# Subtracting query maxima on TensorE, in a reordered attention loop: what it does to a fused attention and spectral-mixing kernel

## The chip, the cores and the metric

The kernel runs on one core of a Trainium2 chip. The metric is device microseconds (us) of one execution. A profiled execution also has a span, from its first to its last instruction, some 1.7 us under its own time. Calls ran on different chips, so a comparison across calls is weaker than one within a call.

## The reference

Condensed:

```python
def phi(x):                                   # q, k: (8, 8, 576, 64); w_phi: (64, 128)
    proj = np.einsum('bhsd,df->bhsf', x, w_phi)
    proj = proj - np.max(np.abs(proj), axis=-1, keepdims=True)
    return np.concatenate([np.exp(proj), np.exp(-proj)], axis=-1)
kv  = einsum(phi(k), v);  z = sum(phi(k))     # per batch and head
x   = (phi(q) @ kv) / (phi(q) @ z + 1e-6)     # heads side by side: (8, 576, 512)
X   = rfft(x, axis=1)[:, :64]                 # 64 modes, each times its own complex 512x512 matrix
u   = x + irfft(mixed X);  out = u + relu(u @ w_ch)
```

The 128 mode matrices (real and imaginary) are 134 MB in HBM as fp32; they are the bulk of what the kernel reads (163.6 MB). Note that `np.exp(-proj)` is taken after the subtraction of the maximum m, so the two halves are exp(p - m) and exp(-p + m). The kernel before makes exp(p) and exp(-p) of the queries and multiplies one of the two sums by exp(2m), as a common factor cancels between numerator and denominator; the changed one makes exp(p - m) and exp(-p + m) directly.

## The kernel before

Attention is cut into 16 units (two heads, two batches each). One unit's work for its queries:

```python
def rows_q(self, i):                # projections, rows on partitions; DVE reduces the absolute maximum
    m = self.mq
    self.rows(self.qT, i, m[:, :, 4 * i:4 * i + 4] if i < 2 else m[:, :, 8])

def exp_mq(self):                   # exp(2m), four small ACT instructions
    self.e2 = pm.tile([128, 2, 9], F32, name="e2")
    ...
def cols_q(self, i): ...            # projections again, features on partitions: two PSUM banks
def exp_q(self, i): ...             # ACT: exp(p) and exp(-p) of them

def num(self, n0):                  # six of 18 row groups; three calls a unit
    pn = [None, None]
    for ab in (1, 0):               # one PSUM group for each sign
        pn[ab] = one([128, 6, 65])
        ... pe.matmul(pn[ab][...], lhsT=AQ, rhs=kvz, start=True, stop=True)
    nd = pm.tile([128, 6, 65], F32, name="nd")
    dve.tensor_tensor(out=nd, in0=pn[1], in1=<e2 broadcast>, op=ALU.mult)
    dve.tensor_tensor(out=nd, in0=pn[0], in1=nd, op=ALU.add)
    dve.reciprocal(rd, nd[:, :, 64])
    dve.tensor_tensor(out=xs[...], in0=nd[:, :, 0:64], in1=<rd broadcast>, op=ALU.mult)
```

The loop runs unit Q (numerators), K (keys' projections, query transposes and maxima) and R (key transposes) at once, and from pass n = 4 on mixes weights in between (condensed):

```python
Q.cols_q(0); Q.exp_q(0); K.rows_k(0); K.exp_k(0)
Q.kv(); Q.cols_q(1); Q.exp_q(1); P.freq()                 # P: spectrum of the unit before Q
if n == 4: some(2)                                        # some(k): k weights' mixing matmuls
Q.num(0); K.turn_q(); K.rows_k(1); K.exp_k(1); some(min(X, 2))
Q.num(6); Q.cols_q(2); Q.exp_q(2); some(min(X - 2, 2))
K.rows_k(2); K.exp_k(2); K.weigh_v(); K.rows_q(0); K.rows_q(1); K.rows_q(2)
R.turn_k(); K.weigh_v2(); Q.num(12); K.exp_mq(); some(X - 4)
```

All engines keep program order. Weights are loaded as bf16 by transfers that GpSimd issues, 1 MB each, into 13 places at first (8 rotating buffers and 5 borrowed tiles); each `some` step that frees a rotating buffer issues the next one:

```python
def wload(g, w):
    wt = home(g, w)                                       # one of the 13 places
    pool.dma_start(wt, (moe_w_r, moe_w_i)[i][MG * o:MG * o + MG, ...])
def some(n):
    for _ in range(n):
        mix(*key, wts.pop(key), ...)                      # 8 matmuls
        if key not in held: next_w(1)                     # the place is free: issue the next weight
```

After attention come the inverse tables (about 20 us of VectorE, PE idle), then the rest of the mixes among channel products and sums, and last the output stage.

Of the kernel before, what the change touches and what calls it, by code (L numbers as in the profile page):

```python
# [10 lines left out]
F32 = mybir.dt.float32  # L11
# [32 lines left out]
def kernel(  # L44
# [42 lines left out]
    pm = pm_cm.__enter__()  # L87

# [8 lines left out]
    class Unit:  # L97
# [15 lines left out]
        def turn(self, src, name, flat):  # L113

            dst = pm.tile([128, 9, 128], BF16, name=name, tag="xT", bufs=3)
            rows = src.rearrange("p i c d -> p (i c d)")
            for lo, hi in ((0, 4), (4, 9)):
                ptr = one([128, hi - lo, 128], BF16)
                for j in range(lo, hi):
                    if flat or j < 4:  # L120
                        pe.transpose(ptr[:, j - lo, :], rows[:, j * 128:(j + 1) * 128], ident_b)
                    elif j < 8:
                        n = 9 + 2 * (j - 4)
                        pe.transpose(ptr[:, j - lo, :], rows[:, n * 64:n * 64 + 128], ident_b)
                    else:
                        for i in range(2):
                            pe.transpose(ptr[64 * i:64 * i + 64, j - lo, :], src[:, i, 8, :], ident_b)
                act.copy(dst[:, lo:hi, :], ptr)
            return dst

        def turn_k(self):
            self.kT = self.turn(self.kb, "kT", True)
            self.mk = pm.tile([128, 2, 18], F32, name="mk")

        def turn_q(self):
            self.qT = self.turn(self.qb, "qT", False)
            self.mq = pm.tile([128, 2, 9], F32, name="mq")
# [21 lines left out]
        def exp_k(self, i):  # L159
            if i == 0:  # L160
                self.AB = []
            if i < 2:
                t = pm.tile([128, 2, 8, 128], BF16, name="AB", bufs=3)
            else:
                t = pm.tile([128, 2, 2, 128], BF16, name="ABr")
            for ab in range(2):
                act.activation(t[:, ab], self.pk, ACT.Exp, scale=1.0 - 2.0 * ab)
            self.AB.append(t)
# [18 lines left out]
        def kv(self):  # L187
            pk = [one([128, 2, 2, 65]) for h in range(2)]
            for i in range(2):
                for ab in range(2):  # L190
                    for c in range(9):
                        n = 9 * i + c
                        for h in range(2):
# [5 lines left out]
                            )  # L199
            for h in range(2):  # L200
                act.copy(self.kvz[:, h], pk[h])

        def rows_q(self, i):
            m = self.mq
            self.rows(self.qT, i, m[:, :, 4 * i:4 * i + 4] if i < 2 else m[:, :, 8])

        def exp_mq(self):
            self.e2 = pm.tile([128, 2, 9], F32, name="e2")
            for h in range(2):
                for a in range(2):  # L210
                    act.activation(self.e2[64 * a:64 * a + 64, h, :], self.mq[64 * h:64 * h + 64, a, :],
                                   ACT.Exp, scale=2.0)

        def cols_q(self, i):

            if i < 2:
                ps = two([128, 2, 4, 128])
                for c2 in range(2):
# [4 lines left out]
                        start=True, stop=True,  # L223
                    )
            else:
                ps = one([128, 2, 128])
                for h in range(2):
                    pe.matmul(ps[:, h, :], lhsT=w2blk[:, h * 128:(h + 1) * 128],
                              rhs=self.qT[:, 8, :], start=True, stop=True)
            self.pa = ps  # L230

        def exp_q(self, i):
            if i == 0:
                self.AQ = []
            if i < 2:
                t = pm.tile([128, 2, 2, 2, 2, 2, 64], BF16, name="AQ")
            else:
                t = pm.tile([128, 2, 2, 128], BF16, name="AQr")
# [9 lines left out]
        def num(self, n0):  # L248

            pn = [None, None]  # L250
            for ab in (1, 0):
                pn[ab] = one([128, 6, 65])
                for n in range(n0, n0 + 6):
                    h = n % 2
                    if n < 16:
                        i, c = n // 8, n % 8 // 2
                        pe.matmul(
                            pn[ab][:, n - n0, :],
                            lhsT=self.AQ[i][:, ab, c % 2, c // 2, h].rearrange("f a p -> f (a p)"),
                            rhs=self.kvz[:, h, i, ab, :], start=True, stop=True,  # L260
                        )
                    else:
                        for i in range(2):
                            r = slice(64 * i, 64 * i + 64)
                            pe.matmul(
                                pn[ab][r, n - n0, :],
                                lhsT=self.AQ[2][:, ab, i, 64 * h:64 * h + 64],
                                rhs=self.kvz[:, h, i, ab, :], start=True, stop=True,
                            )
            nd = pm.tile([128, 6, 65], F32, name="nd")  # L270
            dve.tensor_tensor(
                out=nd.rearrange("p (k h) d -> p k h d", h=2),
                in0=pn[1].rearrange("p (k h) d -> p k h d", h=2),
                in1=self.e2[:, :, n0 // 2:n0 // 2 + 3].rearrange("p h k -> p k h").unsqueeze(3)
                .to_broadcast([128, 3, 2, 65]), op=ALU.mult,
            )
            dve.tensor_tensor(out=nd, in0=pn[0], in1=nd, op=ALU.add)
            rd = pm.tile([128, 6], F32, name="rd")
            dve.reciprocal(rd, nd[:, :, 64])
            dve.tensor_tensor(  # L280
                out=xs[:, self.g, self.bp, n0:n0 + 6, :], in0=nd[:, :, 0:64],
# [3 lines left out]
        def freq(self):  # L285
            g, bp = self.g, self.bp
            px = one([128, 4, 2, 64])
            for i in range(2):
                for c in range(5):
# [5 lines left out]
                    )  # L295
            act.copy(
# [50 lines left out]
    dve.tensor_copy(ident_b, ident_f)  # L347
    units[0].load_q()
# [17 lines left out]
    units[0].turn_k()  # L366
# [83 lines left out]
    units[2].load_k()  # L450
    for n in range(-1, len(units) + 1):
        def unit(i):
            return units[i] if 0 <= i < len(units) else None

# [374 lines left out]
```

## Time and profile before

| what | before |
|---|---|
| time, median of 3 (lowest to highest) | 482.02 us (479.99 to 482.52) |
| span of the profiled run, granted clock | 478.6 us, 0.852 |
| busy: PE, VectorE, ScalarE | 338, 314, 293 us |
| attention ends (first mix after it) | 320.1 us |
| last packet of the last weight | 423.1 us |
| matmuls of the last weight | 434.65 us |

How to read it: there are two things that can set the end. One is the row of work: attention, tables, rest, each as fast as its engines pass work on. The other is the row of transfers, which is nearly full from the start; the last weight must have landed before its matmuls, and what follows those matmuls takes 44 us. In the kernel before the row of work was the later one, by 434.65 - 423.1 = 11.5 us. The last mix has no wait for a weight:

```profile
434.65 0.69 PE L37 MATMUL pt<-wt,XT 128*32 128x512 bf16 x8
```

### The profile page before, as it was taken

How to read it: one execution, taken by the hardware profiler on the slowest of the kernel's cores; microseconds unless marked ns; L12 is line 12 of the kernel's file. 1: busy time of each engine (PE TensorE's matmuls, PEld its weight loads, DVE VectorE, ACT ScalarE, POOL GpSimd, SP SyncE). 2: the span in 40 equal slices, each digit the busy share in tenths (PEclk: the TensorE clock that was granted, in tenths of full speed). 3: DMA queues.
4: the chain of work that ended last, by engine and by line, in shares of the span. 5: the costliest groups of instructions: out<-in, count | busy, mean ns of one | idle time of the engine just before them, and what ended most of it. 6: DMA issues, size and time to landing. Idle time of an engine off the chain costs nothing.

```text
span 478.6 us, 9253 instructions
## 1 busy us (share of the span) xinstructions
PE 337.9 (71%) x3738; PEld 201.4 (42%) x3780; DVE 313.8 (66%) x547; ACT 292.8 (61%) x524; POOL 92.7 (19%) x130
## 2 busy tenths in 40 slices
PE   1566666747776667867877777650499995999991
PEld 1354444535454454544554554430255541333330
DVE  5368768739588778788696696647533331775782
ACT  4566867857769777767658767501244542666671
POOL 5222210104113202212122021050012120000331
PEclk9998888589789888788588597785699997999996
DMA  8999999968999999999999999999999999931797
GB/s 193 207 228 209 227 227 213 222 142 129 229 214 223 228 227 208 229 219 217 228 207 228 228 207 207 205 189 207 207 207 213 214 218 217 207 75 45 216 326 250
DMA packets 86299, 99.23 MB, mean 207 GB/s; under 512 B 2800, under 2 KB 79728, under 8 KB 86256
## 3 DMA queue, kind: packets, MB, share of 16 engines
q0 software_dynamic: 77264, 81.80, 100.0%
q1 hardware_dynamic: 8992, 16.85, 11.2%
q8 instruction: 29, 0.48, 0.4%
q14 instruction: 14, 0.11, 0.1%
HBM read 163.64 MB, written 9.44 MB: 362 GB/s over the span
## 4 chain that ended last, share of the span: by engine, by line
DVE 35%; issue 28%; PE 21%; ACT 7%; POOL 5%; DMA 3%; POOLq 0%; DVEq 0%; ACTq 0%
PE pt L37 12%; DVE va L37 7%; PE one L37 7%; DVE mq L37 7%; DVE mk L37 6%; DVE nd L37 6%; ACT AB L37 4%; DVE xs L37 3%; DMA qb<-in_q_dram 3%; PE two L37 2%; POOL wt L37 2%; POOL out_dram L37 2%; DVE zall L37 2%; ACT kvz L37 2%; DVE rd L37 1%
## 5 line engine op out<-in xcount | busy, mean ns | idle before, releaser
L37 ACT ACTIVATE AB<-two 128x1024 bf16<-128x1024 f32 x64 | 62.0, 1021 | 55.3 <-DVE mk L37 55.3
L37 ACT CAST xw<-pt 128x512 bf16<-128x512 f32 x72 | 42.1, 587 | 44.9 <-PE pt L37 43.8
L37 ACT ACTIVATE AQ<-two 128x1024 bf16<-128x1024 f32 x64 | 62.7, 1043 | 0.7 <-PE two L37 0.3
L37 DVE TENSOR_TENSOR nd<-one,e 128x390 f32<-128x390 f32 x48 | 26.7, 557 | 54.4 <-PE one L37 54.4
L37 PE MATMUL one<-kvz,AQ 128*128 128x65 bf16 x512 | 33.8, 214 | 31.0 <-ACT kvz L37 21.6
L37 PE MATMUL pt<-wchb,xT 128*128 128x512 bf16 x136 | 36.9, 385 | 20.0 <-DVE xT L37 19.7
L37 PE MATMUL one<-va,AB 64*128 64x65 bf16 x1024 | 29.9, 216 | 26.4 <-DVE va L37 26.1
L37 PEld LDWEIGHTS <-AQ 128*128 128x128 bf16 x512 | 28.5, 111 | 45.4 <-issue 43.5
L37 DVE TENSOR_REDUCE mk<-two 128x8 f32<-128x1024 f32 x32 | 39.0, 1220 | 10.1 <-PE two L37 9.9
L37 POOL DMA_DIRECT2D wt<-in_moe_w_r_dram x29 | 25.6, 883 | 85.5 <-PE one L37 63.2
L37 DVE TENSOR_TENSOR va<-vn,ee 128x1152 bf16<-128x1152 f32 x32 | 41.9, 1352 | 0.0
L37 POOL DMA_DIRECT2D qb<-in_q_dram x16 | 11.4, 712 | 154.1 <-PE one L37 154.1
L37 PEld LDWEIGHTS <-AB 64*128 64x128 bf16 x1024 | 25.8, 111 | 32.6 <-DVE va L37 18.0
L37 PEld LDWEIGHTS <-xs 128*128 128x128 bf16 x304 | 29.2, 112 | 24.4 <-issue 11.4
L37 DVE TENSOR_REDUCE mq<-two 128x8 f32<-128x1024 f32 x32 | 37.7, 1217 | 1.4 <-PE two L37 1.4
L37 DVE TENSOR_TENSOR xs<-pt,xs 128x512 bf16<-128x512 f32 x36 | 24.3, 691 | 18.3 <-PE pt L37 17.9
L37 POOL DMA_DIRECT2D wt<-in_moe_w_i_dram x30 | 26.5, 882 | 44.9 <-PE pt L37 43.6
L37 PEld LDWEIGHTS <-XT 128*32 128x32 bf16 x512 | 20.1, 173 | 29.7 <-issue 20.5
L37 PE MATMUL one<-CF,xs 128*128 128x256 bf16 x160 | 29.3, 344 | 4.4 <-DVE xs L37 2.8
L37 DVE COPY xT<-pt 128x512 bf16<-128x512 bf16 x36 | 15.1, 422 | 26.2 <-PE pt L37 26.2
L37 DVE TENSOR_TENSOR nd<-one,nd 128x390 f32<-128x390 f32 x48 | 27.1, 565 | 5.4 <-DVE nd L37 0.5
L37 PE MATMUL one<-wt,XT 128*32 128x512 bf16 x296 | 26.4, 486 | 4.2 <-ACT yacc L37 2.4
(107 smaller groups left out, 652.2 us busy)
## 6 DMA issues: line engine op xcount, KB each, us to landing
wt<-in_moe_w_i_dram POOLq DMA_DIRECT2D x30, 1024.0 KB, 20.9
wt<-in_moe_w_r_dram POOLq DMA_DIRECT2D x29, 1024.0 KB, 18.7
vn<-in_v_dram SPq DMA_DIRECT2D x16, 576.0 KB, 7.6
kb<-in_k_dram POOLq DMA_DIRECT2D x16, 288.0 KB, 20.6
qb<-in_q_dram POOLq DMA_DIRECT2D x16, 288.0 KB, 13.1
out_dram<-of SPq DMA_DIRECT2D x16, 256.0 KB, 5.3
out_dram<-of POOLq DMA_DIRECT2D x16, 256.0 KB, 5.0
yacc<-in_moe_w_r_dram POOLq DMA_DIRECT2D x1, 1024.0 KB, 12.0
```

The source lines that it names most:

```text
L37: ins = f(*args, **kwargs)
```

## The change

The intent is to take work off VectorE. The query maximum is split into three bf16 parts (high 16 bits of m, of the remainder, of its remainder), transposed by TensorE, and subtracted from the projections in PSUM by a matmul with minus one. Both exponentials then carry the right factor, so their two products with the key sums accumulate in one PSUM group, and VectorE only divides. The loop is reordered and starts one pass earlier: query transposes and the first query columns are now made one pass ahead of where they were.

```diff
+        def shift_q(self):
+            high = self.m3.bitcast(BF16).rearrange("p t (n s) -> p t n s", s=2)[:, :, :, 1]
+            for t in range(2):
+                dve.tensor_tensor(out=self.m3[:, t + 1, 0:18], in0=self.m3[:, t, 0:18],
+                                  in1=high[:, t, 0:18], op=ALU.subtract)
+            pt = one([96, 128], BF16)
+            pe.transpose(pt, high.rearrange("p t n -> p (t n)"), ident_b)
+            self.mT = pm.tile([96, 128], BF16, name="mT")
+            act.copy(self.mT, pt)
+        def shifted(self, out, n, stop):
+            pe.matmul(out, lhsT=minus[:, n:n + 1].to_broadcast([96, 128]), rhs=self.mT,
+                      start=False, stop=stop)
         def cols_q(self, i):
...
-                        start=True, stop=True,
+                        start=True, stop=False,
                     )
+                    for j in range(4):
+                        self.shifted(ps[:, c2, j, :], 8 * i + 2 * j + c2, j == 3)
...
         def num(self, n0):
-            (two groups, then nd = pn[1] * e2, nd = pn[0] + nd: see above)
+            pn = one([128, 6, 65])      # ab = 0 starts the group, ab = 1 adds to it
+            dve.reciprocal(rd, pn[:, :, 64])
+            dve.tensor_tensor(out=xs[...], in0=pn[:, :, 0:64], in1=<rd broadcast>, op=ALU.mult)
...
-    for n in range(-1, len(units) + 1):
-        X = 0 if n < 4 else 6 if n == 4 else 4 if n % 2 else 2
+    for n in range(-2, len(units) + 1):
+        X = 0 if n < 4 else 6 if n == 4 else 3 if n % 2 else 2
+        Q.exp_q(0); K.rows_k(0); K.exp_k(0); Q.weigh_v2(); P.freq(); P.keep_x()
+        if n == 4: some(2)
+        Q.cols_q(1); Q.exp_q(1); some(1 if X else 0); K.rows_k(1); K.exp_k(1)
+        Q.kv(); K.rows_q(0); K.rows_k(2); K.rows_q(2); K.rows_q(1)
+        Q.cols_q(2); Q.keep_kv(); Q.exp_q(2); K.exp_k(2); K.weigh_v(); some(1 if X else 0)
+        K.shift_q(); Q.num(0); K.cols_q(0); R.turn_k(0); R.turn_k(1)
+        Q.num(6); R.turn_q(0); R.turn_q(1); Q.num(12); some(X - 2)
+        if n < 3: next_w((1, 3, 3, 2, 2)[n + 2])
```

(The loop is condensed; loads and the guards for missing units are cut.)

More of the change, by code (lines that the diff above doesn't have):

```diff
@@ L87 @@
     pm = pm_cm.__enter__()
+    m3s = [pm.tile([128, 3, 32], F32, name=f"m3{i}", bufs=1) for i in range(2)]
+    minus = pm.tile([96, 32], BF16, name="minus", bufs=1)
     def load(t, src, g, bp, eng):
@@ L111, in load_v, with turn @@
             load(self.vn, v, self.g, self.bp, sp)
-        def turn(self, src, name, flat):
-            dst = pm.tile([128, 9, 128], BF16, name=name, tag="xT", bufs=3)
+        def turn(self, src, dst, flat, part):
             rows = src.rearrange("p i c d -> p (i c d)")
-            for lo, hi in ((0, 4), (4, 9)):
-                ptr = one([128, hi - lo, 128], BF16)
-                for j in range(lo, hi):
-                    if flat or j < 4:
-                        pe.transpose(ptr[:, j - lo, :], rows[:, j * 128:(j + 1) * 128], ident_b)
-                    elif j < 8:
-                        n = 9 + 2 * (j - 4)
-                        pe.transpose(ptr[:, j - lo, :], rows[:, n * 64:n * 64 + 128], ident_b)
-                    else:
-                        for i in range(2):
-                            pe.transpose(ptr[64 * i:64 * i + 64, j - lo, :], src[:, i, 8, :], ident_b)
-                act.copy(dst[:, lo:hi, :], ptr)
-            return dst
@@ L131, in turn_k @@
-        def turn_k(self):
-            self.kT = self.turn(self.kb, "kT", True)
-            self.mk = pm.tile([128, 2, 18], F32, name="mk")
-        def turn_q(self):
-            self.qT = self.turn(self.qb, "qT", False)
-            self.mq = pm.tile([128, 2, 9], F32, name="mq")
+            lo, hi = ((0, 4), (4, 9))[part]
+            ptr = one([128, hi - lo, 128], BF16)
+            for j in range(lo, hi):
+                if flat or j < 4:
+                    pe.transpose(ptr[:, j - lo, :], rows[:, j * 128:(j + 1) * 128], ident_b)
+                elif j < 8:
+                    n = 9 + 2 * (j - 4)
+                    pe.transpose(ptr[:, j - lo, :], rows[:, n * 64:n * 64 + 128], ident_b)
+                else:
+                    for i in range(2):
+                        pe.transpose(ptr[64 * i:64 * i + 64, j - lo, :], src[:, i, 8, :], ident_b)
@@ new lines, in turn, with turn_k, turn_q @@
+            act.copy(dst[:, lo:hi, :], ptr)
+        def turn_k(self, part):
+            if part == 0:
+                self.kT = pm.tile([128, 9, 128], BF16, name="kT", bufs=2)
+                self.mk = pm.tile([128, 2, 18], F32, name="mk")
+            self.turn(self.kb, self.kT, True, part)
+        def turn_q(self, part):
+            if part == 0:
+                self.qT = pm.tile([128, 9, 128], BF16, name="qT", bufs=3)
+                self.m3 = m3s[self.bp % 2]
+            self.turn(self.qb, self.qT, False, part)
@@ L164, in exp_k @@
             else:
-                t = pm.tile([128, 2, 2, 128], BF16, name="ABr")
+                t = pm.tile([128, 2, 2, 128], BF16, name="ABr", bufs=1)
             for ab in range(2):
@@ L199, in kv, with keep_kv @@
                             )
+            self.pk2 = pk
+        def keep_kv(self):
             for h in range(2):
-                act.copy(self.kvz[:, h], pk[h])
+                act.copy(self.kvz[:, h], self.pk2[h])
         def rows_q(self, i):
-            m = self.mq
-            self.rows(self.qT, i, m[:, :, 4 * i:4 * i + 4] if i < 2 else m[:, :, 8])
-        def exp_mq(self):
-            self.e2 = pm.tile([128, 2, 9], F32, name="e2")
-            for h in range(2):
-                for a in range(2):
-                    act.activation(self.e2[64 * a:64 * a + 64, h, :], self.mq[64 * h:64 * h + 64, a, :],
-                                   ACT.Exp, scale=2.0)
+            self.rows(self.qT, i, self.m3[:, 0, 8 * i:min(8 * i + 8, 18)])
+        def shift_q(self):
[10 more added lines that the diff above has]
+                      start=False, stop=stop)
         def cols_q(self, i):
@@ L228, in cols_q @@
                     pe.matmul(ps[:, h, :], lhsT=w2blk[:, h * 128:(h + 1) * 128],
-                              rhs=self.qT[:, 8, :], start=True, stop=True)
+                              rhs=self.qT[:, 8, :], start=True, stop=False)
+                    self.shifted(ps[:, h, :], 16 + h, True)
             self.pa = ps
@@ L235, in exp_q @@
             if i < 2:
-                t = pm.tile([128, 2, 2, 2, 2, 2, 64], BF16, name="AQ")
+                t = pm.tile([128, 2, 2, 2, 2, 2, 64], BF16, name="AQ", bufs=3)
             else:
-                t = pm.tile([128, 2, 2, 128], BF16, name="AQr")
+                t = pm.tile([128, 2, 2, 128], BF16, name="AQr", bufs=1)
             for ab in range(2):
@@ L248, in num @@
         def num(self, n0):
-            pn = [None, None]
-            for ab in (1, 0):
-                pn[ab] = one([128, 6, 65])
-                for n in range(n0, n0 + 6):
-                    h = n % 2
-                    if n < 16:
-                        i, c = n // 8, n % 8 // 2
+            pn = one([128, 6, 65])
+            for n in range(n0, n0 + 6):
+                h = n % 2
+                if n < 16:
+                    i, c = n // 8, n % 8 // 2
+                    for ab in range(2):
@@ L257, in num @@
                         pe.matmul(
-                            pn[ab][:, n - n0, :],
+                            pn[:, n - n0, :],
                             lhsT=self.AQ[i][:, ab, c % 2, c // 2, h].rearrange("f a p -> f (a p)"),
-                            rhs=self.kvz[:, h, i, ab, :], start=True, stop=True,
+                            rhs=self.kvz[:, h, i, ab, :], start=(ab == 0), stop=(ab == 1),
                         )
-                    else:
-                        for i in range(2):
-                            r = slice(64 * i, 64 * i + 64)
+                else:
+                    for i in range(2):
+                        r = slice(64 * i, 64 * i + 64)
+                        for ab in range(2):
@@ L265, in num @@
                             pe.matmul(
-                                pn[ab][r, n - n0, :],
+                                pn[r, n - n0, :],
                                 lhsT=self.AQ[2][:, ab, i, 64 * h:64 * h + 64],
-                                rhs=self.kvz[:, h, i, ab, :], start=True, stop=True,
+                                rhs=self.kvz[:, h, i, ab, :], start=(ab == 0), stop=(ab == 1),
                             )
-            nd = pm.tile([128, 6, 65], F32, name="nd")
+            rd = pm.tile([128, 6], F32, name="rd")
@@ L271, in num @@
+            dve.reciprocal(rd, pn[:, :, 64])
             dve.tensor_tensor(
-                out=nd.rearrange("p (k h) d -> p k h d", h=2),
-                in0=pn[1].rearrange("p (k h) d -> p k h d", h=2),
-                in1=self.e2[:, :, n0 // 2:n0 // 2 + 3].rearrange("p h k -> p k h").unsqueeze(3)
-                .to_broadcast([128, 3, 2, 65]), op=ALU.mult,
-            )
-            dve.tensor_tensor(out=nd, in0=pn[0], in1=nd, op=ALU.add)
-            rd = pm.tile([128, 6], F32, name="rd")
@@ L279, in num @@
-            dve.reciprocal(rd, nd[:, :, 64])
-            dve.tensor_tensor(
-                out=xs[:, self.g, self.bp, n0:n0 + 6, :], in0=nd[:, :, 0:64],
+                out=xs[:, self.g, self.bp, n0:n0 + 6, :], in0=pn[:, :, 0:64],
                 in1=rd.unsqueeze(2).to_broadcast([128, 6, 64]), op=ALU.mult,
@@ L295, in freq, with keep_x @@
                     )
+            self.px = px
+        def keep_x(self):
+            g, bp, px = self.g, self.bp, self.px
             act.copy(
@@ L347 @@
     dve.tensor_copy(ident_b, ident_f)
+    for t in range(3):
+        r = slice(32 * t, 32 * t + 32)
+        dve.tensor_scalar_mul(out=minus[r], in0=ident_f[r, r], scalar1=-1.0)
+    for m3 in m3s:
+        dve.memset(m3, 0.0)
     units[0].load_q()
@@ L364, in clear @@
             dve.memset(x[:, i:i + 2], 0.0)
-    units[0].turn_k()
     clear(XTb[0])
@@ L449, with unit @@
     units[1].load_q()
-    units[2].load_k()
-    for n in range(-1, len(units) + 1):
-        def unit(i):
-            return units[i] if 0 <= i < len(units) else None
+    def unit(i):
+        return units[i] if 0 <= i < len(units) else None
+    for n in range(-2, len(units) + 1):
         P, Q, K, R = (unit(n + i) for i in (-1, 0, 1, 2))
-        X = 0 if n < 4 else 6 if n == 4 else 4 if n % 2 else 2
+        X = 0 if n < 4 else 6 if n == 4 else 3 if n % 2 else 2
         if Q:
-            Q.cols_q(0)
             Q.exp_q(0)
@@ L463 @@
         if Q:
-            Q.kv()
-            Q.cols_q(1)
-            Q.exp_q(1)
+            Q.weigh_v2()
+            if unit(n + 2):
+                unit(n + 2).load_v()
         if P:
             P.freq()
+            P.keep_x()
             if P.bp == NP - 1:
@@ L473 @@
         if Q:
+            Q.cols_q(1)
+            Q.exp_q(1)
+        some(1 if X else 0)
+        if K:
+            K.rows_k(1)
+            K.exp_k(1)
+        if Q:
+            Q.kv()
+        if K:
+            K.rows_q(0)
+            K.rows_k(2)
+            K.rows_q(2)
+            K.rows_q(1)
+        if Q:
+            Q.cols_q(2)
+            Q.keep_kv()
+            Q.exp_q(2)
+        if K:
+            K.exp_k(2)
+            K.weigh_v()
+        some(1 if X else 0)
+        if K:
+            K.shift_q()
+        if Q:
             Q.num(0)
         if K:
-            K.turn_q()
-            if unit(n + 3):
-                unit(n + 3).load_q()
-            K.rows_k(1)
-            K.exp_k(1)
-        if n < 3:
-            next_w((2, 2, 2, 2)[n + 1])
-        some(min(X, 2))
+            K.cols_q(0)
+        if R:
+            R.turn_k(0)
+            R.turn_k(1)
+            if unit(n + 4):
+                unit(n + 4).load_k()
         if Q:
             Q.num(6)
-            Q.cols_q(2)
-            Q.exp_q(2)
-        some(min(X - 2, 2))
-        if K:
-            K.rows_k(2)
-            K.exp_k(2)
-            K.weigh_v()
-            K.rows_q(0)
-            K.rows_q(1)
-            K.rows_q(2)
         if R:
-            R.turn_k()
+            R.turn_q(0)
+            R.turn_q(1)
             if unit(n + 4):
-                unit(n + 4).load_k()
-        if K:
-            K.weigh_v2()
-            if unit(n + 3):
-                unit(n + 3).load_v()
+                unit(n + 4).load_q()
         if Q:
             Q.num(12)
-        if K:
-            K.exp_mq()
+        some(X - 2)
         if n == -1:
             forward_table()
-        if n < 2:
-            next_w((1, 2, 0)[n + 1])
-        some(X - 4)
+        if n < 3:
+            next_w((1, 3, 3, 2, 2)[n + 2])
         if n == 6:
```

## The prediction

> **What bounds the kernel now.** I read the page first, then the waits, the timeline of each engine over one unit, and the table of stretches. The busy line and the slices come first.
>
> ```profile
> PE 337.9 (71%) x3738; PEld 201.4 (42%) x3780; DVE 313.8 (66%) x547; ACT 292.8 (61%) x524; POOL 92.7 (19%) x130
> ...
> PE   1566666747776667867877777650499995999991
> ...
> PEclk9998888589789888788588597785699997999996
> DMA  8999999968999999999999999999999999931797
> ```
>
> No engine is full over the span. The PE row shows three stages: attention at six to eight tenths up to slice 26 (about 320 us), a hole in slices 27 and 28 (VectorE makes the inverse tables, no matmul from 324 to 336 us), then a PE-bound rest with 9s. The DMA row is full nearly everywhere, so the first question is whether weight transfers set the end. The table of stretches (PE, PEld, DVE, ACT, POOL busy with counts, clock, DMA share, GB/s) answers it.
>
> ```profile
> 96.00:102.00 6.00, 3.01 (x83) 2.09 (x76) 3.94 (x6) 3.12 (x5) 0.00 (x0) 1.00 1.18 239
> 102.00:108.00 6.00, 2.99 (x33) 1.72 (x34) 0.48 (x1) 3.54 (x7) 0.00 (x0) 0.74 0.11 34
> 108.00:114.00 6.00, 3.63 (x58) 2.64 (x56) 5.49 (x12) 4.18 (x7) 1.61 (x2) 0.98 0.54 75
> ...
> 420.00:426.00 6.00, 5.87 (x32) 2.25 (x33) 3.84 (x7) 3.96 (x8) 0.00 (x0) 1.00 0.51 111
> 426.00:432.00 6.00, 6.00 (x39) 2.13 (x38) 4.63 (x7) 4.36 (x8) 0.00 (x0) 1.00 0.00 0
> ```
>
> The transfers run full (share about 1.2) up to 422 us, but for a dip of some 9.5 us at 102 to 114: the 13 weights that have a place before the first mix have landed, and the next is issued only when a mix frees one. The last weight lands near 422 us and the timeline has its matmuls at 434.65, so weights arrive 12 us early, and the waits list no wait of PE for a weight. Transfers are full, yet they do not set the end. They are the next limit: without the dip they would end near 412, and the 44 us from the last mix to the end (478.6 - 434.7) give a **transfer floor** of about 456 us of span, or 460 in the times, which are some 3.4 us above this span (482.0 against 478.6).
>
> So attention's pace decides. Units without mixes follow each other at 17.6 us (rk0, the reduction of a unit's first key rows, starts at 28.3, 46.3, 63.8, 81.4 in the chain); with three mixes on average a unit takes 18.3 (158.2 to 249.7 is five units, 91.5 / 5). DVE, ACT and PE in turn, in one unit:
>
> ```profile
> 59.21 2.62 DVE L37 TENSOR_TENSOR va<-vn,ee 128x1152 bf16<-128x1152 f32 x2
> 61.74 0.55 DVE L37 TENSOR_TENSOR nd<-one,e 128x390 f32<-128x390 f32 x1
> 62.40 0.56 DVE L37 TENSOR_TENSOR nd<-one,nd 128x390 f32<-128x390 f32 x1
> ...
> 63.70 1.22 DVE L37 TENSOR_REDUCE mk<-two 128x8 f32<-128x1024 f32 x1
> 68.03 0.56 DVE L37 TENSOR_TENSOR nd<-one,e 128x390 f32<-128x390 f32 x1 [3.11 <-PE one L37]
> ```
>
> ```profile
> 64.95 1.94 ACT L37 ACTIVATE AB<-two 128x1024 bf16<-128x1024 f32 x2 [2.88 <-DVE mk L37]
> 66.78 0.66 ACT L37 CAST kvz<-one 128x260 bf16<-128x260 f32 x2
> 67.30 1.98 ACT L37 ACTIVATE AQ<-two 128x1024 bf16<-128x1024 f32 x2
> ```
>
> ```profile
> 67.21 1.04 PE L37 MATMUL one<-kvz,AQ 128*128 128x65 bf16 x12 [2.54 <-ACT kvz L37]
> 68.06 1.42 PE L37 MATMUL one<-ident_b,qb 128*128 128x128 bf16 x10
> 69.41 1.03 PE L37 MATMUL two<-w2blk,kT 128*128 128x256 bf16 x4
> ```
>
> It is a ring through all three engines, each idle while another works: va 2.6, the last third of the numerators on DVE 2.0, rk0 1.2, AB 1.9, kvz 0.4, numerator matmuls 0.85, query transposes 1.35, key rows 1.0, rk1 1.2, second third on DVE 2.0, the small key reduction 0.5, three query reductions 2.8. The sum is 17.8, against 17.6 seen. Adding durations without gaps therefore describes this loop, and I use the same method below.
>
> **What the Trainium skill says.** "PSUM — Partial Sum Buffer", section Terms: two engines on one bank and quadrant at once are a collision, "reads against reads included". That explains why ACT's key exponential, which does not need mk, waits for its reduction; the trace agrees (AB idles 55.3 us behind mk), and the change keeps this order. "TensorE: Matmul & The Clock Gate", section Part 1: the array clock halves after an idle window and recovers after sustained work. The trace agrees: key rows x4 take 0.60 us when PE was busy and 1.03 after a gap, and PEclk moves between 0.5 and 1 during attention. "Perfetto Trace Analysis", section Optimizing Scalar/DVE Operations: a fixed access cost per instruction, about doubled in the profiled latency. The trace agrees: a 9-column ACT exponential takes 210 ns and a 6-column reciprocal 192 ns, so I take 0.2 us for each small new instruction.
>
> **The change part by part**, per unit.
> Removed from DVE: six nd instructions, 3 x 0.557 + 3 x 0.565 = 3.4 us. Removed from ACT: four e exponentials, 0.88 us as a group. Added to DVE: two subtractions of 18 columns, 0.4. Added to ACT: one copy of the transposed maxima, about 0.25. Added to PE: one transpose and 18 matmuls of 128 columns, with weight load each; nine such transposes take 0.67 us warm (74 ns each) and ten take 1.42 cold, so 1.3 to 2.6 us. Reciprocal and division now read PSUM; I leave them at 0.19 and 0.56. Numerator matmuls keep their number.
> Busy sums per unit: DVE 14.2 (56.8 / 4 over 163.8 to 236.7 us) to 11.2; ACT 13.3 to 12.7; PE 13.4 at three mixes to about 14.6. None sets 17; order does.
>
> New order, laid out by hand with the durations above. Time zero is the first query exponential: two exponentials of query and key 1.96 + 1.94, the spectrum copy 0.5, the second query exponential 1.95: 6.35. That frees a double bank; query rows 0.8 gives 7.15. DVE reduces 1.22 + 0.4 + 0.4 + 1.17: 10.35. Negation and two subtractions: 10.9; transpose 11.1. Then PE in program order: six numerators 0.9, shifted query columns 1.3, key transposes 0.8, six numerators 0.85, query transposes 0.95: 15.9. The last query copy ends 0.75 later: **16.7 us against 17.6**. DVE's weighting of V and most of its division now lie beside other work, so the 3.4 us saved are worth only 0.9. With mixes: two go where PE is idle; every second one puts a 0.69 us yacc addition ahead of the subtractions, so about 17.1 against 18.3.
>
> Sum: the ramp is even (query transposes now precede the first key rows, and the first full unit starts near 29 us as before). Units 0 to 3 save 4 x 0.9 = 3.6 us, and 11 later ones 1.2 each, some 13. That is 17. The loop now mixes 38 weights instead of 42 (2 or 3 a unit, not 2 or 4), so four mixes of 0.69 us go to the PE-bound rest: +2.8. Net about -14 us: 482 - 14 = 468.
>
> **Rivals.**
> 1. PE takes the place of DVE. The chain holds five PE pieces in a row (4.8 us), and an 18-matmul block: at half clock this is 2.5 to 4 us more and the unit stays at 17.6 or over. For it: clock 0.8 in attention and PE gaps near 2 us. Against: PE gets more work, so it may stay warmer. It gives 480 to 487.
> 2. Transfers become the bound. A unit needs 2.5 x 5.06 us of weights (1.05 MB at the 207 GB/s seen when only weights move) and about 4.4 us of keys, queries and values: 17.0 us. If the loop ran at 15 us, mixes would wait for weights and the end would stick at the floor, 460 to 466. Against: my 17.1 is just not faster than transfers.
> 3. The dip stays hidden or grows. In the first unit with mixes the new order mixes four of eight weights only at its end, so the issue resumes late; I expect 5 to 7 us of dip. With 12 us of spare time this should cost nothing, which makes "same" only if the loop gains nothing either.
> 4. PSUM single banks run short: two for keys times values, one held by a mix pair, and one for the small rows; a wait for the kvz copy sits there at about 8.7 us of the unit. I count 0.2 us; 1 us a unit would cancel the gain.
>
> **Range and chances.** An error of 0.6 us per unit over 16 units is 10 us. Below stands the floor near 460, which I may have 2 us too high; above, rival 1. So 468, from 458 to 483. Faster by over 2% means under 472.4: 0.6. Slower means over 491.7, some 1.5 us a unit (24 / 16) more than laid out: 0.05. Same: 0.35.
>
> **What would show it.** Right: no e or second nd group; DVE busy falls by about 48 us (16 x 3.0); first-key reductions of successive units 16.5 to 17.3 us apart; attention ending near 305 us; ACT waiting at the turn of the unit for PE transposes; dip under 8 us; last mix near 421. Wrong: if PE waits for wt transfers or the last landing is within 3 us of its mix, rival 2; if new minus matmuls run over 120 ns each and the clock is under 0.75, rival 1; if PE waits on kvz or banks stay over 1 us a unit, rival 4.

## More of the kernel before

A call's verdict is "same" or "faster" by a margin of 2%, and "unclear" where the runs do not decide.

The profiled run itself took 480.39 us, 1.8 us over its span.

## The result, and the profile after

The changed kernel took 465.66 us (median of 4, 464.38 to 468.84) against 481.0 (476.91 to 482.52). Executions over 1.5% slower than the fastest of the same kernel are left out of the means. A ratio in this document is the mean time of one kernel's fast runs over that of the other's of the same rounds, so not quite the ratio of the medians quoted: here 0.9704, 95% interval 0.9624 to 0.9784. It is faster, and the time is 2.3 us from the one predicted. The traces compared below are of single runs, before 480.39 us and after 468.84, the slowest of its four: they differ by 11.5 us where the medians differ by 15.3.

The page of the kernel after, the same lines as before (busy time, then the slices):

```profile
PE 337.8 (72%) x4084; PEld 207.5 (44%) x4084; DVE 269.1 (58%) x488; ACT 281.1 (60%) x475; POOL 92.7 (20%) x130
...
PE   0377677758788777788768778129997656997991
...
DMA  8999999999999999999999999999999999992797
```

VectorE lost 313.8 - 269.1 = 44.7 us. The hole of the tables has moved from slices 27 and 28 (counted from 0) to 25 and 26. Behind it PE had one slice of 5 among 9s before; now it falls after three slices to 7, 6, 5 and 6. Attention ended much earlier than the time gained: the first mix after attention stands at 292.2 us instead of 320.1, 27.9 us sooner, and the span is only 11.5 us shorter. The waits of PE, which listed no weight before, and the last mix in the timeline, say where the rest stayed:

```profile
PE pt L37 <- DMA wt<-in_moe_w_i_dram: 9.9, 4, 3.0
PE pt L37 <- DMA wt<-in_moe_w_r_dram: 2.9, 3, 1.2
```

```profile
422.94 0.67 PE L37 MATMUL pt<-wt,XT 128*32 128x512 bf16 x8 [1.67 <-DMA wt<-in_moe_w_i_dram]
```

PE now waits 12.8 us in seven pieces for weights, and the last mix begins as its weight lands: its last packet ends at 422.6 us, against 423.1 in the kernel before. The last landing moved by 0.5 us only. The gain between these two traces, 11.5 us, is the 11.5 us by which weights used to be early.

Transfers still have their hole, in the stretches where the kernel before had it (columns as in the prediction: PE, PEld, DVE, ACT, POOL, clock, DMA share, GB/s):

```profile
102.00:108.00 6.00, 2.81 (x50) 1.95 (x43) 4.57 (x8) 4.11 (x10) 0.78 (x1) 0.95 0.86 163
108.00:114.00 6.00, 6.00 (x94) 5.01 (x96) 2.26 (x6) 2.74 (x7) 1.72 (x4) 0.76 1.03 161
```

It is shallower (against a full share of 1.22 they lose 6 x 0.36 / 1.22 = 1.8 and 6 x 0.19 / 1.22 = 0.9 us; the next stretch and one at 30 to 36 us lose 0.4 and 1.1), and by 400 us the kernel has moved 85.4 MB where the kernel before had moved 84.4. But that lead, worth some 5 us at 207 GB/s, was nearly gone at the last packet. One thing beside it can be read from the trace: from 408 to 416 us the changed kernel also moves 0.52 MB of mixed modes (`yl`, issued at 404.78 and 407.67 us; at 419.03 and 421.92 in the kernel before), and only 1.13 MB of weights, where the kernel before moves 1.65 MB of weights. The 0.52 MB are an estimated 2.5 us of weights; no run moves them later, so that they cost time is not shown. The tail is also longer: of the last 1024 weight packets (as many as one weight has; a packet does not name its weight) half had ended by 416.5 us and the last ended 6 us later (418.1 and 5 us before). Why they straggle is open.

One unit without mixes, the row that the prediction laid out by hand. DVE and ACT first, then PE:

```profile
70.73 1.23 DVE L37 TENSOR_REDUCE m<-two 128x8 f32<-128x1024 f32 x1
71.87 0.17 DVE L37 TENSOR_SCALAR mk<-mk 128x18 f32<-128x18 f32 x1
71.99 0.39 DVE L37 TENSOR_TENSOR m<-m 128x18 f32<-128x18 f32 x2
```

```profile
75.28 1.20 ACT L37 COPY qT<-one 128x512 bf16<-128x512 bf16 x2
76.34 1.99 ACT L37 ACTIVATE AQ<-two 128x1024 bf16<-128x1024 f32 x2
```

```profile
72.43 0.26 PE L37 MATMUL one<-ident_b,m 128*96 128x128 bf16 x1 [1.51 <-DVE m L37]
72.53 0.54 PE L37 MATMUL one<-kvz,AQ 128*128 128x65 bf16 x12
72.90 0.38 PE L37 MATMUL two<-qT,w2blk 128*128 128x512 bf16 x1
73.12 0.39 PE L37 MATMUL two<-mT,minus 96*128 96x128 bf16 x4
73.34 0.38 PE L37 MATMUL two<-qT,w2blk 128*128 128x512 bf16 x1
73.56 0.39 PE L37 MATMUL two<-mT,minus 96*128 96x128 bf16 x4
73.79 0.67 PE L37 MATMUL one<-ident_b,kb 128*128 128x128 bf16 x9
74.29 0.54 PE L37 MATMUL one<-kvz,AQ 128*128 128x65 bf16 x12
74.67 0.78 PE L37 MATMUL one<-ident_b,qb 128*128 128x128 bf16 x10
75.44 0.41 PE L37 MATMUL one<-kvz,AQ 128*128 128x65 bf16 x8
```

The row is the one laid out: last query reduction, two subtractions, transpose, six numerators, shifted columns, key transposes, six numerators, query transposes, copy, next query exponential. It is faster than laid out. From the first six numerators to the end of the query transposes PE takes 75.44 - 72.53 = 2.9 us, not 4.8, and this unit takes 14.3 us (the exponential AQ that opens a unit starts at 62.07 and 76.34), not 16.7. It is one of the two fastest: the four units without mixes take 17.0, 14.2, 14.3 and 15.8 us (first key reductions at 31.4, 48.4, 62.6, 76.9 and 92.7), 15.3 on average against 17.6.

### The profile page after: what moved, and what is told of

Its sections match the earlier page's. It is cut to its first block, busy times and chain, and to the rows that moved or that the text cites. A ratio compares the mean times of both kernels' runs of the same rounds, so it can differ in the third digit from the quotient of the medians.

```text
span 467.1 us, 9757 instructions
## 1 busy us (share of the span) xinstructions
PE 337.8 (72%) x4084; PEld 207.5 (44%) x4084; DVE 269.1 (58%) x488; ACT 281.1 (60%) x475; POOL 92.7 (20%) x130
## 4 chain that ended last, share of the span: by engine, by line
issue 37%; DMA 21%; PE 16%; ACT 8%; POOL 8%; DVE 7%; POOLq 0%; ACTq 0%
PE pt L37 8%; DMA wt<-in_moe_w_r_dram 8%; DMA wt<-in_moe_w_i_dram 6%; DMA kb<-in_k_dram 5%; PE one L37 4%; POOL wt L37 4%; PE two L37 4%; DVE m L37 4%; ACT AQ L37 3%; DMA qb<-in_q_dram 3%; POOL out_dram L37 2%; ACT AB L37 2%; DVE zall L37 2%; ACT qT L37 1%; ACT kT L37 1%
## 5 line engine op out<-in xcount | busy, mean ns | idle before, releaser
L37 DVE TENSOR_REDUCE m<-two 128x8 f32<-128x1024 f32 x32 | 39.2, 1224 | 19.4 <-PE two L37 19.3
L37 POOL DMA_DIRECT2D wt<-in_moe_w_r_dram x29 | 25.6, 881 | 95.7 <-PE one L37 62.0
L37 DVE RECIPROCAL rd<-one 128x6 f32<-128x6 f32 x48 | 9.4, 196 | 50.3 <-PE one L37 50.3
L37 ACT COPY kT<-one 128x512 bf16<-128x512 bf16 (+1 forms) x32 | 19.2, 640 | 30.0 <-PE one L37 30.0
L37 PEld LDWEIGHTS <-minus 96*128 96x128 bf16 x288 | 27.4, 114 | 20.1 <-issue 14.8
L37 PE MATMUL two<-qT,w2blk 128*128 128x512 bf16 x64 | 29.9, 467 | 6.3 <-ACT AQ L37 6.3
L37 PE MATMUL two<-w2blk,qT 128*128 128x256 bf16 x128 | 21.2, 292 | 16.5 <-ACT AB L37 11.9
L37 DVE COPY xT<-pt 128x512 bf16<-128x512 bf16 x36 | 15.1, 422 | 27.9 <-PE pt L37 27.9
L37 PE MATMUL two<-mT,minus 96*128 96x128 bf16 x256 | 30.3, 252 | 0.0
L37 PE MATMUL pt<-wt,XT 128*32 128x512 bf16 x208 | 18.6, 434 | 13.6 <-DMA wt<-in_moe_w_i_dram 9.9
L37 PEld LDWEIGHTS <-qT 128*128 128x128 bf16 x144 | 14.4, 103 | 31.3 <-issue 28.4
L37 DVE TENSOR_TENSOR xs<-one,rd 128x384 bf16<-128x384 f32 x48 | 26.8, 558 | 1.6
## 6 DMA issues: line engine op xcount, KB each, us to landing
kb<-in_k_dram POOLq DMA_DIRECT2D x16, 288.0 KB, 17.6
```

What stands on the lines that cost most here:

```text
L37: ins = f(*args, **kwargs)
```

## The experiments

Where a name ends in "half", half of every weight is loaded and used twice, a wrong computation; it still passes the comparison with the reference, because the mixed modes are small in the output. This takes the transfers out of the question and leaves all other work as it was:

```diff
-            wt, (moe_w_r, moe_w_i)[i][MG * o:MG * o + MG, g * 128:(g + 1) * 128, :].rearrange(
+            wt[:, 0:4], (moe_w_r, moe_w_i)[i][MG * o:MG * o + 4, g * 128:(g + 1) * 128, :].rearrange(
...
-                    rhs=wt[:, 4 * t + j, :], ...
+                    rhs=wt[:, j, :], ...
```

### Before and after with half weights: who is held by transfers

> The kernel before with half of every weight loaded and used twice (wrong result on purpose), so that weight transfers halve and nothing else changes. Theory (before was held by its attention loop, weights came 12 us early): 476 to 482 us, units still about 17.6 us apart. Rival (before was already held by transfers): 30 us or more faster.

> The changed kernel with half of every weight. Theory (its loop ends 27 us earlier, but the last weights hold the end, so 12 to 15 us of the gain are lost there): 450 to 457 us, that is some 25 us under the kernel before with half weights, and no wait of PE for a weight. Rival (the rest of the gain is lost in the stage after attention, by more mixes there and the clock): it stays at 462 to 467 us.

Before with half weights: 477.95 us (4 runs), ratio 0.9957 to the kernel before on the same chip, interval 0.9884 to 1.003: the same. So the kernel before was not held by transfers. After with half weights: 452.33 us (449.74 to 453.8), ratio 0.9426; PE waits for no weight, and its last mix stands at 403.4 us, before the 422.6 at which the last whole weight had landed. So the change is worth 477.95 - 452.33 = 25.6 us of work, and whole weights let some 15 of them through. The rest is not lost in the stage after attention as such; it is lost there waiting for weights. The granted clock, which rose from 0.852 to 0.904 with the change, does not explain the gain: of the next two runs one has 0.871 and no gain, the other 0.869 and all of it.

### The two parts of the change apart

The new arithmetic in the old order, with the splitting and transposing of the maxima put where the old kernel made its factor exp(2m), at the end of a pass:

```diff
-            K.exp_mq()
+            K.shift_q()          # with the new rows_q, cols_q and num
```

> The new arithmetic alone, in the old order, half weights. Theory of the ring of durations: the two thirds of the division that stand in the old ring shrink from 2.0 to 0.8 us each, the transpose and its copy add some 0.3, so a unit takes 15.4 to 15.8 us instead of 17.6 and the time is about 450 to 458. Rival (the saved VectorE work is worth nothing without the new order): 474 to 482.

It took 484.69 us, ratio 1.0101 (interval 1.0031 to 1.0171): the same by the 2% margin, no gain at all, if anything 1% slower. My expectation was missed. The timeline of DVE and of PE shows the reason:

```profile
74.20 0.41 DVE L37 TENSOR_REDUCE m<-one 128x2 f32<-128x256 f32 x1
74.53 0.24 DVE L37 CAST va<-ee 128x36 bf16<-128x36 f32 x1
74.62 2.62 DVE L37 TENSOR_TENSOR va<-vn,ee 128x1152 bf16<-128x1152 f32 x2
77.16 0.19 DVE L37 RECIPROCAL rd<-one 128x6 f32<-128x6 f32 x1
77.38 0.56 DVE L37 TENSOR_TENSOR xs<-one,rd 128x384 bf16<-128x384 f32 x1
77.86 0.38 DVE L37 TENSOR_TENSOR m<-m 128x18 f32<-128x18 f32 x2
```

```profile
78.29 0.34 PE L37 MATMUL one<-ident_b,m 128*96 128x128 bf16 x1 [3.35 <-DVE m L37]
```

The maxima are complete at 74.6 us, but the two short subtractions, 0.38 us together, stand behind the weighting of V and a division, so PE idles 3.35 us before the transpose; such waits occur 16 times, 69.8 us in all ("PE one <- DVE m" in the waits). In this place the shift is a new wait that eats what it saves. So the next run moves it to where its input is ready:

```diff
             K.rows_q(2)
+            K.shift_q()
...
-            K.shift_q()          # no longer at the end of the pass
```

> The new arithmetic in the old order, half weights, but the subtractions and the transpose stand right after the query reductions and not at the unit's end. Theory (the arithmetic alone lost because the transpose waited behind the weighting of V and the last third of the division, 4 us of PE idle a unit): units 15 to 16 us apart, 450 to 462 us, near the changed kernel with half weights. Rival (the saved work needs the new order wherever the transpose stands): 470 us or more.

It took 452.29 us (450.64 to 452.51): 0.04 us from the changed kernel with half weights (another chip), without the new order. In its timeline the subtractions come directly behind the last query reduction and ahead of the weighting of V:

```profile
69.78 0.41 DVE L37 TENSOR_REDUCE m<-one 128x2 f32<-128x256 f32 x1
70.23 0.39 DVE L37 TENSOR_TENSOR m<-m 128x18 f32<-128x18 f32 x2
70.54 0.24 DVE L37 CAST va<-ee 128x36 bf16<-128x36 f32 x1
```

Against 477.95 the same arithmetic costs 6.7 us or gains 25.7, by the place of two instructions in VectorE's order and of the transpose behind them. In that call one run of the kernel before was 473.84 us, and by it five others at 481 to 482 counted as slow; I therefore compare medians across calls here and not the ratio (0.9451, interval 0.9392 to 0.9511, verdict "unclear").

The reverse, the new order with the old arithmetic (with one buffer for the weighted sum instead of two, to fit):

```diff
-            K.shift_q()
+            K.exp_mq()           # with the old rows_q, cols_q and num, in the new order
```

> The new order alone, with the old arithmetic (exponential of the maxima, two groups and their weighted sum; one buffer for that sum instead of two, for room), half weights. Theory: six more sums a unit put VectorE's work at the end of a unit on the path, 16.3 to 17.2 us a unit, 460 to 472 us. Rival (the order is all of the gain): as the changed kernel with half weights, 450 to 457.

463.96 us, ratio 0.9681: 14.0 us of the 25.6 come from the order alone, as expected. Parts do not add: 14.0 for the order, 25.7 for the arithmetic well placed, 25.6 for both. Spacing of units says more (first copy of the key sums of successive units): the second and third unit without mixes took 17.6 us before, 15.9 with the order alone, 16.5 with the arithmetic well placed, and 14.2 and 14.3 with both (14.2 and 15.8 in the changed kernel's trace with half weights); with mixes, from the seventh to the fifteenth unit, 18.3, 17.4, 16.7 and 16.4 (all but the first with half weights). The order does win in units without mixes. It gives that back elsewhere: its first copy of key sums comes at 35.7 us instead of 29.2, and it leaves four mixes more to the end. Once the shift is well placed, the order adds nothing to the time that these runs show.

### The parts with whole weights

> The new order alone with the old arithmetic and whole weights. Its loop with half weights gave 464 us, near the 466 to 469 us at which the transfers hold the changed kernel. Theory (the end is the later of the two): 467 to 473 us, so that with whole weights nearly all of the gain is to be had without the new arithmetic. Rival (losses of both kinds add up): 476 us or more.

474.19 us, ratio 0.9874 (interval 0.9839 to 0.9909; "same" by the 2% margin, though clear of 1), somewhat over the range expected. The last mix waits for its weight and is at 425.8 us, so the transfers hold this one too:

```profile
425.79 0.68 PE L37 MATMUL pt<-wt,XT 128*32 128x512 bf16 x8 [1.40 <-DMA wt<-in_moe_w_i_dram]
```

What I had not counted is that a kernel also sets its own last landing. This one's hole is deeper: shares of 0.38 and 0.62 at 102 to 114 us, that is 6 x 0.84 / 1.22 + 6 x 0.60 / 1.22 = 7.1 us lost, against 2.7 in the changed kernel. Its first transfer into a freed place is issued at 109.1 us, against 107.2 in the changed kernel.

> The new arithmetic in the old order, transpose right after the query reductions, whole weights. Theory (with half weights it equals the changed kernel, and with whole weights the last landing plus 44 us sets both): 464 to 470 us, as the changed kernel, PE waiting for weights in the last stage or in the loop. Rival (its loop takes three weights a unit, so it starves differently): 474 us or more.

465.46 us, ratio 0.9689 (0.9652 to 0.9725): as the changed kernel's 465.66 and 0.9704, in the old order. The rival's time did not come, though this loop does wait differently: 3.6 us once for a weight within it, and 4.2 us after it.

### The end follows the last landing

Three versions of one call on one chip, five rounds: the changed kernel again; the same with all eight first mixes as soon as their spectrum is there, so that their places are free sooner; and that with one weight issued a pass earlier in the ramp.

```diff
-        X = 0 if n < 4 else 6 if n == 4 else 3 if n % 2 else 2
+        X = 0 if n < 5 else 3 if n % 2 else 2
...
             if n == 4:
-                some(2)
+                some(8)
...
-            next_w((1, 3, 3, 2, 2)[n + 2])       # second version only
+            next_w((2, 3, 3, 2, 1)[n + 2])
```

> The changed kernel unchanged, on the chip of the next two runs, to compare them with: 464 to 469 us, PE waiting some 10 to 13 us for weights in the last stage.

> The changed kernel with all eight first mixes at once when their spectrum is there, in place of two, one, one and four over the unit: weights are issued again some 5 to 15 us sooner, so most of the 3 us of transfer time lost at 102 to 120 us comes back. Theory (transfers hold the end): 2 to 4 us faster than the changed kernel on the same chip. Rival (they do not, and the burst of eight mixes only delays the unit): same or up to 3 us slower.

> As the run with the early mixes, and one weight is issued one step earlier in the ramp (2, 3, 3, 2, 1 in place of 1, 3, 3, 2, 2), which fills the hole of transfers at 30 to 36 us, about 1.1 us. Theory: another 0.5 to 1.5 us, 3 to 5 us under the changed kernel. Rival: no difference, or the earlier weight delays a load of keys or queries in the ramp and costs 1 to 3 us.

Medians: 469.45 (465.8 to 470.38), 464.19 (463.13 to 465.4) and 462.0 (461.14 to 463.35). On this chip the changed kernel's own ratio to the kernel before is 0.98 (interval 0.9737 to 0.9862), "unclear" by the 2% margin: a smaller gain than the first measurement's. So the early mixes are worth 5.3 us and the earlier weight 2.2, both more than expected; part of the first may be that the changed kernel's profiled run in this call lost more in its hole (shares 0.67 and 0.77) than in the first one. With the early mixes the hole is gone (shares 1.23 and 1.24), and so it is in the last version, where the earlier weight also closes the one at 30 to 36 us (1.24 instead of 1.10):

```profile
102.00:108.00 6.00, 4.36 (x103) 3.44 (x100) 3.33 (x5) 4.91 (x7) 3.17 (x4) 1.00 1.18 250
108.00:114.00 6.00, 4.51 (x77) 3.80 (x78) 3.67 (x11) 4.37 (x11) 1.41 (x2) 1.00 1.24 208
```

```profile
416.60 0.67 PE L37 MATMUL pt<-wt,XT 128*32 128x512 bf16 x8 [0.91 <-DMA wt<-in_moe_w_i_dram]
```

In these three profiled runs the last mix is at 423.96, 417.60 and 416.60 us and the span 468.6, 461.6 and 460.1: the difference is 44.6, 44.0 and 43.5. The end follows the landing of the last weight nearly one to one. This last version computes the reference in full and is the fastest that does: ratio 0.9663, and its median is 7.5 us under the changed kernel's on the same chip.

> The same with all eight first mixes at once. Theory (the hole of transfers after the first four units closes, the end follows the last landing): 460 to 465 us, as the best version so far (462), without the new order. Rival (the new order is worth something once transfers are denser): 467 us or more.

The old order with the well-placed shift and early mixes: 464.33 us (463.88 to 465.51), only 1.1 us under the same without early mixes, though within the range expected, and 0.1 us from the new order with the same early mixes (464.19, another chip). Its stretch at 102 to 108 us still has a share of 0.59. The matmuls of its fourth unit's spectrum begin at 97.6 us and the first transfer into a freed place is issued at 104.1; in the new order with early mixes these are at 89.3 and 97.5, and at 94.4 and 100.8 in the fastest version. The old order has the spectrum later in a pass, behind the key sums. So in the new order transfers go on sooner after the first four units, and the trace shows the smaller hole; a gain in time from it is not shown, as the two times are equal. What sets the fastest version apart is the weight issued earlier in the ramp, and no run tries that in the old order.

### What the subtracting matmuls cost

```diff
         def shifted(self, out, n, stop):
-            pe.matmul(out, lhsT=minus[:, n:n + 1].to_broadcast([96, 128]), rhs=self.mT,
-                      start=False, stop=stop)
+            pass
```

(The projections before them then end their group with stop=True.)

> The changed kernel with half weights and without the 18 subtracting matmuls a unit (maxima still reduced, transposed and copied; the result stays right only because the factor cancels in numerator over denominator and these inputs are small, so it is no version to use). Theory: eight of them, 55 ns each when warm, lie in the row of PE pieces on the path, so 0.4 to 0.9 us a unit, 6 to 14 us in all: 438 to 446 us against 452. Rival (they lie beside other work): 449 to 453 us.

441.67 us against 452.33 with them (another chip; the kernel before was at 480.8 and 479.0 there), ratio 0.9177 against 0.9426: some 10.7 to 12 us, or 0.7 a unit, for 18 matmuls that take 55 ns each from start to start in the row above (four of them from 73.12 to 73.34). That is not their pace everywhere: over the changed kernel's trace the time from one's start to the next start on PE has a median of 59 ns, a quarter take 107 or more, and the mean is 81 where no gap over 0.3 us follows. Eight lie in the row above: 0.44 us at 55 ns, and an estimated 0.65 at 81. No run tells whether that is where the 0.7 comes from.

## Why the prediction was right or wrong

The time was right, 465.66 us against 468, by luck: two errors met. Its mechanism was right in part.

- **What bounds the kernel before.** Right: halved transfers leave it the same (0.9957).
- **Removed and added work.** Right: VectorE's busy time fell by 44.7 us against 48 predicted; ScalarE's by 11.7.
- **The row of a unit.** The row itself was right, its size wrong: 15.3 us a unit without mixes on average and 14.3 in the one shown above, not 16.7; with mixes 16.7 (first key reductions from 133.2 to 267.0 us, eight units), not 17.1. The term that failed is "Then PE in program order: six numerators 0.9, shifted query columns 1.3, key transposes 0.8, six numerators 0.85, query transposes 0.95", 4.8 us in all, measured 2.9. I had taken durations of groups from the kernel before, where PE had gaps (clock 0.72 from 66 to 78 us there, 1.00 from 60 to 84 us in the kernel after), and added durations of groups that overlap: twelve numerators are listed at 0.54 us, and the next work starts 0.37 us after them. ScalarE's pairs too: listed at 1.99, the next starts 1.81 later.
- **Attention's gain.** Wrong in size: 27.9 us, not 17; it ended at 292 us, not 305. The row's size is only a part of it. By the first key reductions, the four units without mixes give 9.3 us, where 3.6 were laid out, and the ten units that follow give 13.9, near the 13 laid out for eleven. "The ramp is even" is wrong: the first full unit starts at 31.4 us instead of 28.3, a loss of 3.1. And the way from the last of these reductions to the first mix after attention shrank from 33.0 to 25.2 us, 7.8, of which the prediction had only the four mixes of 0.69.
- **"Transfers are full, yet they do not set the end."** True of the kernel before and wrong of the one after. This is rival 2, and the prediction's own signs for it (waits of PE for weights, last landing within 3 us of its mix) were seen; so was its time, 460 to 466. Only the mixes waited after attention and not in the loop. In the two traces it kept 16 of the 27.9 us.
- **The floor.** Named, but put at 460 in the times, as if the hole were filled ("without the dip they would end near 412"). The changed kernel filled part of it, yet its last packet came at 422.6; the floor that held in the trace was 423 + 44 = 467 of span, not 456. (The step from span to time was 3.4 us in the prediction, a median less the span of a faster run; the profiled runs have 1.7 to 1.8. The dip, by the shares, was 8.8 us and not 9.5.) With the hole closed by experiment the time is 462.0. So two errors met: attention was 11 us better than laid out, and the floor 11 us of span higher than reckoned, and the sum landed close.
- **Rival 1** (PE in VectorE's place) did not happen: subtracting matmuls had a median of 59 ns, not over 120, and the clock was 0.904 over the run. **Rival 3** expected a hole of 5 to 7 us: it was 2.7 us at 102 to 114 us (4.9 by the same shares in the changed kernel's second trace), and it was wrong that it costs nothing: mixing early, which closed it, gave 5.3 us. **Rival 4**: PE waits 8.9 us in all on the copy of key sums, half a microsecond a unit, under the 1 us named.

## What to carry to other kernels

Work out both rows to the end, that of work and that of transfers, and know the slack between them: a change to the work pays about that slack (11.5 us here, in the traces), after which only what lets the last transfer land earlier pays. When arithmetic moves to another engine, place the short instructions that the other engine waits for directly behind their input in program order; here two subtractions of 0.2 us each and the transpose behind them, placed wrongly, cost some 32 us (484.69 against 452.29, on two chips). And when a row is added up from a profile, take start-to-start times from a stretch at the clock that the changed kernel will have (1.00 here), not durations from a slower one (0.72).

## What the Trainium skill lacked or had wrong

- "TensorE: Matmul & The Clock Gate", section Back-to-back issue gap, gives about 81 ns a matmul at N = 128 for a stream of weight loads and matmuls. Here four subtracting matmuls of 128 columns, each with its own weight load, take 0.22 us from start to start, 55 ns each, at a granted clock of 1.00; that is near the 56 ns which the section gives for an isolated gap. Over the whole run the median is 59 ns.
- The same page, Part 4, says of transposes that some 275 ns were seen in a kernel's context and that the full clock does not engage for them. Here nine in a row, among other matmuls, take 0.50 us from start to start (73.79 to 74.29), 56 ns each, at a granted clock of 1.00; a single one is listed at 0.26 us, so the page's figure is near the listed duration of one and is not the pace of a row.
- "DMA: Bandwidth & Descriptors", section Where 436 GB/s comes from, has the HBM side bind at about 358 GB/s a core, and in the same paragraph a measurement of 425. In stretches with weights alone the trace has 207 GB/s written as bf16; as they are read as fp32, that is an estimated 414 GB/s read by this one core, over the first figure and under the second.
- No page tells how far the engines' shares of one transfer spread at the end of a long full queue: of the sixteen signals with which the last 1 MB weight reports its landing, the first came at 416.9 us and the last at 422.9 (419.9 and 423.4 in the kernel before).
